# Decode block on one Trainium2 core: output in four transfers, GpSimd as closer, later load of x, spare matmuls

## Chip, cores, metric

One core of one Trainium2 chip runs the whole program. The metric is the device time in microseconds of one execution, as the median of several. The core's span in the profile is about 1.8 us shorter than the reported time. The update records of before show nearly every semaphore being written between 989.07 and 989.72 us, after the last instruction; that these writes make up the difference was not tested.

A transfer has three moments in what follows: its issue (an instruction on SyncE or ScalarE that starts it), its packets (moved by the 16 DMA engines), and its landing (the last update of the semaphore that tells the others that the data are there). In the profile lines PE is TensorE and PEld its weight loads, DVE is VectorE, ACT ScalarE, POOL GpSimd; SPq and ACTq are the issues of SyncE and ScalarE.

## The reference

One decode step of a transformer block with four sequences: attention over a cache of 4096 positions and 32 heads of 192, then a gated feed-forward layer.

```python
x = A_x                                              # [4, 1, 640]
h  = x + A_ref(layernorm(x), k_cache, v_cache, wq, wo)   # 32 heads, caches of 4 x 32 x 4096 x 192 bf16
h2 = h + B_ref(layernorm(h), w_gate, w_up, w_down)       # silu(x @ w_gate) * (x @ w_up) @ w_down
return h2                                            # [4, 1, 640] bf16
```

The two caches are 403 of the 424 MB that the kernel reads (4 x 32 x 4096 x 192 elements of two bytes, twice). The profile below shows that these loads set the time.

## The kernel before

The program is written as lists of operations for each engine with semaphore waits worked out from dependencies. Only its two ends matter here. At the start, x is loaded from ScalarE's queue while SyncE starts the first big load, wq:

```python
xd = dma("act", lambda e: e.dma_start(x16[:, :], x[:, 0, :].rearrange("b (n d) -> (b n) d", n=4)), S_x)
c1 = op("pool", ...)          # GpSimd: r32, then identF (c2), then masks
...                           # (cut) layer norm of x on VectorE, TensorE, ScalarE
wq_land = dma("sp", ... wqsb <- wq ..., S_wq)          # 7.9 MB, the first of the long stream on SyncE's queue
...                           # (cut) k and v of 32 units, then wo, w_gate, w_up, w_down, all on SyncE's queue
```

At the end come gate, up and down matmuls, each four column strips of 32 wide, then a cast out of PSUM and the output in two transfers of eight rows:

```python
for k, w in enumerate((wgsb, wusb)):
    for c in range(CD):                       # 5 column blocks; up arrives in two loads, 0-2 and 3-4
        for n in range(4):
            a = op("pe", ... PB[k][32*n:32*n+32, 0:FQ] += lnT[:, c, :].T @ w[:, c, n*FQ:(n+1)*FQ] ...)
    ...                                       # (cut) silu on ScalarE after gate
...                                           # (cut) product and transpose on VectorE -> guT
for c in range(CF):                           # 12 blocks; w_down arrives in three loads, 0-5, 6-9, 10-11
    for n in range(4):
        a = op("pe", ... psH[32*n:32*n+32, 0:DQ] += guT[:, c, :].T @ wdsb[:, c, n*DQ:(n+1)*DQ] ...)
a = op("dve", lambda e: e.tensor_copy(out=outsb[:, 0:DQ], in_=psH[:, 0:DQ]), [a])
fin = [dma(eng, lambda e, n=n: e.dma_start(
    out[:, 0, n * DQ:(n + 2) * DQ].rearrange("b (n d) -> n b d", n=2),
    outsb[32 * n:32 * n + 64:RB, 0:DQ]), S_out, [a]) for n, eng in ((0, "sp"), (2, "act"))]
with nc.Block(no_gpsimd_drain=True) as block:
    pr.emit(block, "act", fin[-1:])           # ScalarE waits for the output's semaphore, then all meet
```

The whole kernel may be printed here:

## Time and profile before

| | |
|---|---|
| time before, first three runs | 990.31 us median (990.21 to 990.85) |
| span of the profiled run | 988.36 us |
| HBM read | 424.29 MB |
| first data packet, last landing of w_down | 1.76 us, 985.01 us |

From the page of the kernel before: the DMA row (share of time in which the 16 DMA engines were busy, in tenths of 40 slices), and the DMA queue's totals.

```profile
DMA  9999999999999999999999999999999999999997
...
q1 hardware_dynamic: 10522, 424.29, 99.5%
...
HBM read 424.29 MB, written 0.01 MB: 429 GB/s over the span
```

The 16 engines are 90% busy or more in every slice but the last; the packets of queue q1 take 99.5% of their span. No compute engine is above 59% of the span. So a saving in the middle of the program should be worth little; the start of the stream and what follows its last byte are what can change the time.

The chain of waits of the kernel before, its last pieces in order (start us, duration us, what):

```profile
947.66 37.35 DMA wd_sb<-in_B_w_down_dram
985.01 0.04 issue
985.06 0.48 PE pb L573 x6
985.54 0.02 issue
985.57 0.33 DVE gu L576
```

The down weights land at 985.01, and only then can the last matmuls run. The chain as shown stops at the cast (L576), 2.5 us before the span's end. What comes after it are transfers, which the chain does not follow. They have to be read elsewhere: the issues from the timeline, here those of the kernel before (start, duration, engine, line),

```profile
985.92 0.68 SPq L577 DMA_DIRECT2D out_dram<-gu  x1
985.92 1.38 ACTq L577 DMA_DIRECT2D out_dram<-gu  x1
```

and packets and landings from the trace's records of DMA packets and of semaphore updates. That gives the tail of the kernel before, in three pieces that lead from the last landing of w_down to the end of the span:

| piece | us |
|---|---|
| last landing of w_down (985.01) to end of cast (985.89) | 0.88 |
| end of cast to last output landing (987.88) | 1.99 |
| last output landing to end of span (988.36) | 0.47 |

The middle piece is the longest, and its data are 5 KB. SyncE's first output packet moves 1.27 us after its issue began.

The stretches of the tail in the kernel before (stretch in us, its length, busy us and instructions of PE, PEld, DVE, ACT and POOL, then the granted TensorE clock, the DMA share and GB/s):

```profile
977.10:980.50 3.40, 1.33 (x16) 0.44 (x20) 0.00 (x0) 0.34 (x1) 0.00 (x0) 0.51 1.02 419
980.50:984.00 3.50, 1.64 (x32) 0.70 (x24) 1.41 (x2) 0.00 (x0) 0.00 (x0) 0.50 0.86 345
984.00:985.60 1.60, 1.18 (x24) 0.54 (x24) 0.03 (x1) 0.00 (x0) 0.00 (x0) 0.50 0.07 29
```

TensorE is busy less than half of each of the first two, and its clock is half (0.50) through the end. The clock records of this trace, which begin at 28.24 us, change only in steps of 3.413 us; these steps are called windows here. By the share of a window covered by matmul records, the 128 windows at full clock that were followed by full clock had 0.57 or more, and the 35 that were followed by half clock 0.54 or less. At half clock the 34 that were followed by full clock had 0.78 or more; the 84 others had 0.75 or less, but for one of 0.82.

### The profile page before, as it was taken

What the parts mean: (1) busy time and instruction counts of PE and PEld (TensorE: products, weight loads), DVE (VectorE), ACT (ScalarE), POOL (GpSimd) and SP (SyncE); (2) the same over time, 40 slices, a digit from 0 to 9 for tenths busy, and PEclk for the clock granted to TensorE, in tenths of its full rate; (3) what the DMA queues carried; (4) which work ended last, traced back from release to release, by engine and by line L of the source; (5) the groups of instructions that cost most, each with busy time, mean ns of one, the idle gap of its engine ahead of it and who ended that gap; (6) DMA issues with size and microseconds to landing.
All of it is one profiled execution on the core that took longest, in us unless ns stands there. A gap on an engine that the chain in (4) does not pass through costs nothing.

```text
span 988.4 us, 9462 instructions
## 1 busy us (share of the span) xinstructions
PE 581.5 (59%) x4409; PEld 128.6 (13%) x2941; DVE 552.6 (56%) x447; ACT 117.1 (12%) x376; POOL 3.6 (0%) x18
## 2 busy tenths in 40 slices
PE   1777555676555567545556654546765555675554
PEld 0001011111011111001111110111110111110023
DVE  1487545566655556655556665555666555566521
ACT  0311111100111110111111011111001111101120
POOL 1000000000000000000000000000000000000000
PEclk9788778887777888777788777778877778877776
DMA  9999999999999999999999999999999999999997
GB/s 403 426 440 424 438 436 428 436 430 436 436 428 438 430 434 436 428 438 432 432 436 428 438 432 432 436 428 438 432 432 436 428 438 434 430 436 428 440 429 327
DMA packets 10571, 424.39 MB, mean 429 GB/s; under 512 B 1220, under 2 KB 1220, under 8 KB 1732
## 3 DMA queue, kind: packets, MB, share of 16 engines
q1 hardware_dynamic: 10522, 424.29, 99.5%
q8 instruction: 5, 0.08, 0.0%
q10 hardware_dynamic: 42, 0.01, 0.0%
q14 instruction: 2, 0.02, 0.0%
HBM read 424.29 MB, written 0.01 MB: 429 GB/s over the span
## 4 chain that ended last, share of the span: by engine, by line
DMA 67%; PE 18%; DVE 12%; issue 1%; SPq 1%; DVEq 0%
DMA k<-in_A_k_cache_dram 64%; DVE prod L413 12%; PE pb L161 11%; PE pb L463 4%; DMA wd_sb<-in_B_w_down_dram 4%; PE pb L421 2%; SPq L366 0%; DVE sc L426 0%; PE pb L469 0%; DVEq L413 0%; SPq L392 0%; SPq L386 0%; PE pb L573 0%; PE pb L435 0%; SPq L331 0%
## 5 line engine op out<-in xcount | busy, mean ns | idle before, releaser
L413 DVE TENSOR_TENSOR prod<-k,qball 128x6144 f16<-128x6144 bf16 x128 | 426.4, 3352 | 220.1 <-DMA k<-in_A_k_cache_dram 220.1
L161 PE MATMUL pb<-prod,identH 128*128 128x512 f16 x1408 | 386.0, 431 | 0.0
L421 PE MATMUL pb<-prod,identH 128*128 128x512 f16 x128 | 57.9, 452 | 337.5 <-DVE prod L413 337.5
L426 DVE TENSOR_REDUCE sc<-pb 128x32 f32<-128x512 f32 x128 | 88.1, 688 | 108.7 <-PE pb L161 108.7
L478 ACT ACTIVATE otmp<-pb,minv 128x192 f32<-128x192 f32 x32 | 13.5, 421 | 649.1 <-PE pb L463 649.1
L421 PEld LDWEIGHTS pb<-prod,identH 128*128 128x128 f16 x128 | 13.2, 103 | 585.3 <-DVE prod L413 472.4
L463 PE MATMUL pb<-v,pbuf 128*8 128x384 bf16 x1984 | 86.0, 326 | 0.0
L454 ACT ACTIVATE pbuf<-sc,negM 32x128 bf16<-32x128 f32 x128 | 73.4, 574 | 4.9
L463 PEld LDWEIGHTS pb<-v,pbuf 128*8 128x8 bf16 x1984 | 45.4, 86 | 28.8
L482 DVE SCALAR_TENSOR_TENSOR orow<-pb,minv,otmp 128x192 f32<-128x192 f32 x32 | 13.4, 418 | 53.7 <-ACT otmp L478 53.7
L498 PEld LDWEIGHTS pb<-orow,here 128*128 128x128 f32 x256 | 33.5, 191 | 73.5 <-issue 71.1
L498 PE MATMUL pb<-orow,here 128*128 128x48 f32 x256 | 31.7, 267 | 1.1 <-DVE orow L482 1.1
L454 ACT ACTIVATION_READ_ACCUMULATOR pbuf<-sc,negM 32x1 f32 x128 | 31.8, 248 | 0.0
L448 ACT ACTIVATE negM<-pb 128x4 f32<-128x4 f32 x32 | 5.6, 174 | 160.2 <-PE pb L444 160.2
L469 PEld LDWEIGHTS pb<-lsb,headm 128*128 128x128 f32 x64 | 12.3, 194 | 74.8 <-issue 71.1
L444 PE MATMUL pb<-negMc,ones_row 1*128 1x4 f32 x64 | 12.2, 258 | 11.8 <-DVE negMc L439 11.8
L435 PE MATMUL pb<-identF,msb 128*1 128x128 f32 x64 | 12.1, 271 | 9.8 <-DVE msb L431 9.8
L439 DVE TENSOR_REDUCE negMc<-pb 1x4 f32<-1x128 f32 x32 | 8.9, 278 | 15.1 <-PE pb L435 15.1
L444 PEld LDWEIGHTS pb<-negMc,ones_row 1*128 1x128 f32 x64 | 9.4, 182 | 21.2 <-DVE negMc L439 21.2
L469 PE MATMUL pb<-lsb,headm 128*128 128x1 f32 x64 | 9.2, 213 | 2.7 <-ACT pbuf L454 2.7
L491 ACT ACTIVATE here<-place 128x131 f32 (+1 forms) x32 | 10.0, 312 | 0.9
L338 PE MATMUL pb<-wq_sb,lnT 128*32 128x384 bf16 x20 | 2.7, 520 | 12.1 <-DMA wq_sb<-in_A_wq_dram 12.1
(65 smaller groups left out, 91.1 us busy)
## 6 DMA issues: line engine op xcount, KB each, us to landing
k<-in_A_k_cache_dram SPq DMA_DIRECT2D x32, 6144.0 KB, 39.5
v<-in_A_v_cache_dram SPq DMA_DIRECT2D x31, 6144.0 KB, 25.5
wq_sb<-in_A_wq_dram SPq DMA_DIRECT2D x1, 7680.0 KB, 21.5
k<-in_A_v_cache_dram SPq DMA_DIRECT2D x1, 6144.0 KB, 39.8
wo_sb<-in_A_wo_dram SPq DMA_DIRECT2D x1, 5760.0 KB, 24.1
wo_sb<-in_A_wo_dram SPq DMA_DIRECT2D x1, 1920.0 KB, 26.1
wg_sb<-in_B_w_gate_dram SPq DMA_DIRECT2D x1, 1920.0 KB, 30.3
wu_sb<-in_B_w_up_dram SPq DMA_DIRECT2D x1, 1152.0 KB, 32.6
```

What stands on the lines that cost most here:

```text
L161: return e.add_instruction(mybir.InstMatmult(name=e.bass.get_next_instruction_name(), engine=mybir.EngineType.PE, start_tensor_calc=start, ...
L413: op("dve", lambda e: e.tensor_tensor(out=prod[BUF[k]][:, :, :], in0=kslot[u % 2][:, k * QT:(k + 1) * QT, :], in1=qball[:, bass.ds(u + pr. ...
L421: op("pe", lambda e, j=j: (e.matmul if j == 0 else partial(held_matmul, e))(psR[k][:, 0:QT * R], lhsT=identH[:, :], rhs=prod[BUF[k]][:, :, ...
L426: op("dve", lambda e: e.tensor_reduce(sc[u % 2][:, k * QT:(k + 1) * QT], psR[k][:, 0:QT * R].rearrange("q (t r) -> q t r", r=R), AX.X, ALU ...
L435: op("pe", lambda e: e.matmul(psS[0:1, XT], lhsT=msb[:, 0:1], rhs=identF[:, :], start=True, stop=True), [g("rmax", u), g("negM", u - 1), p ...
L444: op("pe", lambda e: e.matmul(psS[:, XB], lhsT=ones_row[0:1, :], rhs=negMc[0:1, :], start=True, stop=True), [g("hmax", u), g("negM", u - 1 ...
L454: op("act", lambda e, h=h, r=r: e.activation(out=pbuf[r, :, h], in_=sc[u % 2][r, :], func=ACTF.Exp, bias=negM[r, h:h + 1], scale=alpha, ac ...
L463: op("pe", lambda e, t=t, n=n: e.matmul(psO[32 * n:32 * n + 8, 0:2 * DH], lhsT=pbuf[:, t:t + 2, :].rearrange("q t m -> q (t m)"), rhs=vsrc ...
L469: op("pe", lambda e: e.matmul(psS[:, XL], lhsT=headm[:, :, :].rearrange("q r m -> q (r m)"), rhs=lsb[:, :], start=True, stop=True), [g("ex ...
L478: op("act", lambda e: e.activation(out=otmp[:, :], in_=psO[:, 0:DH], func=ACTF.Copy, scale=minv[:, 0:1]), [g("pv", u), g("minv", u), g("st ...
L482: op("dve", lambda e: e.scalar_tensor_tensor(out=orow[:, :], in0=psO[:, DH:2 * DH], scalar=minv[:, 1:2], in1=otmp[:, :], op0=ALU.mult, op1 ...
L498: op("pe", lambda e, i=i: e.matmul(psT[:, bass.ds(JW * at_unit(u)[0], JW)], lhsT=here[:, NI - 1 - i:NI - 1 - i + 128], rhs=orow[:, JW * i: ...
```

## The change

Four ideas. Smaller output transfers, so that each is done sooner, on two queues. GpSimd instead of ScalarE closes the program, since it collects the other engines at the end anyway (in the trace of before it takes over from ScalarE at 988.17 and lets the others go from 988.25). x waits until the identity matrix is built, which its first use needs too, and leaves the start of the stream to wq. Spare matmuls, whose results nobody reads, fill TensorE's waits so that its clock comes back to full before the last real ones.

```diff
-    xd = dma("act", ... x ..., S_x)
+    xd = dma("act", ... x ..., S_x, [lambda: c2])
...
+    def idle(n):
+        for _ in range(n):
+            op("pe", lambda e: e.matmul(PB[2][:, 0:256], lhsT=sel[:, 0, :], rhs=sel[:, 0:2, :].rearrange("q b m -> q (b m)"),
+                                        start=True, stop=True), [tk["rsum", NU - 1, NQ - 1]])
     for k, w in enumerate((wgsb, wusb)):
         for c in range(CD):
+            if c == 3 and k == 1:
+                idle(2)
...
+        idle(6 if k else 3)
...
     for c in range(CF):
+        if c == 6:
+            idle(3)
...
-    fin = [dma(eng, lambda e, n=n: e.dma_start(
-        out[:, 0, n * DQ:(n + 2) * DQ].rearrange("b (n d) -> n b d", n=2),
-        outsb[32 * n:32 * n + 64:RB, 0:DQ]), S_out, [a]) for n, eng in ((0, "sp"), (2, "act"))]
+    fin = [dma("sp" if n < 2 else "act", lambda e, n=n: e.dma_start(
+        out[:, 0, n * DQ:(n + 1) * DQ], outsb[32 * n:32 * n + 32:RB, 0:DQ]), S_out, [a]) for n in range(4)]
...
-        pr.emit(block, "act", fin[-1:])
+        pr.emit(block, "pool", fin[-1:])
```

More of the change, by code (lines that the diff above doesn't have):

```diff
@@ L270, in g @@
         return tk[key] if key[1] >= 0 else None
-    xd = dma("act", lambda e: e.dma_start(x16[:, :], x[:, 0, :].rearrange("b (n d) -> (b n) d", n=4)), S_x)
+    xd = dma("act", lambda e: e.dma_start(x16[:, :], x[:, 0, :].rearrange("b (n d) -> (b n) d", n=4)), S_x, [lambda: c2])
     c1 = op("pool", lambda e: e.memset(r32[:, :], 0.0))
```

## The prediction

> **What bounds the kernel.** The DMA stream. The page gives 424.39 MB at 429 GB/s; queue q1 is 99.5% of the 16 engines' span. In the packet records a 61,440-byte packet takes 2.267 us on every engine, 27.1 GB/s, so 424.39 MB need 978.8 us; the first packet starts at 1.76 us, the last w_down packet ends near 984.6, practically without idle. Compute counts only after the last landing. The chain of waits ends "DMA wd_sb"; the last w_down landing is 985.01. Then (timeline): eight down matmuls to 985.52, CAST to 985.90, output issues at 985.92 (SyncE 0.68 us, ScalarE 1.38 us), first output packets 987.19 (SyncE) and 987.46 (ScalarE), last landing 987.88, ScalarE's closing steps to 988.14, GpSimd's barrier, end at 988.4. The reported time is 1.8 us longer than the span. The change can touch only this 3.4 us tail and the start of the stream.
>
> **The steps.**
>
> 1. x after the identity. Its issue moves from 0.75 to about 3.1 us (identF ends 3.07). x lands at perhaps 9 to 10 us instead of 8.36; the layer norm takes 3.6 us and wq lands only at 22.3, so nothing waits. But the 16 engines start wq raggedly, from 1.76 to 3.21 us[...], and w_down's last chunk lands equally spread, 983.60 to 985.01[...].[...] Without x in between the last engine should start about 0.5 us sooner; I count -0.4 us on the critical path.
>
> 2. Spare matmuls (14 of 256 columns). The clock records change in steps of 3.413 us; the tail ran at half clock from 977.1. In this trace a window at full clock stayed there at 57% busy or more and fell at 54% or less; at half clock about 80% was needed to rise. The tail's windows had 34, 41, 46 and 35%. A spare costs about 0.21 us cold: three after gate bring 34% only to about 41%; the later ones may lift 46% over 80%. So full clock may return for the last down matmuls only, depending on the phase. Gain at most 0.2 us, on average 0.1. Risk: three cold spares (0.64 us) before column 6 start at 983.8 and delay its matmuls (984.28) by 0.1 to 0.2 us. Net -0.05.
>
> 3. Four output transfers. Four rows each instead of eight, but each queue issues twice, in series. ScalarE's 1.38 us look like waiting for SyncE's. A plain issue took 0.39 to 0.43 us elsewhere. If that holds here, the second pair starts 0.4 us later and the last landing slips: +0.15 us (range -0.3 to +0.8). The least certain term.
>
> 4. GpSimd closes. Saves ScalarE's branch, drain and hand-over (987.91 to 988.17): -0.15 us.
>
> Sum: -0.45 us, 989.8 us, range 988.9 to 990.6. Faster by over 2%: 0.5%; within 2%: 99%; slower: 0.5%.
>
> **What would show it.** Step 1: spread of first wq packets below 1.45 us, last w_down landing before 985.0. Step 2: clock after 975 us; time from last w_down landing to CAST, now 0.55 us. Step 3: CAST end to last output landing, now 1.98 us. Step 4: last landing to end of span, now 0.48 us.
>
> **What would make it wrong.** The ragged start may not come from x; an instruction fetch (16 KB packets[...]) may hit the latest engine; four issues may serialise at 0.7 us each and add a microsecond; the clock windows are phased differently in every run.

The four terms (-0.4, -0.05, +0.15, -0.15) sum to -0.45 us. The instruction fetch at 1.91 us in before took 1.28 us. The 0.21 us of a spare at half clock is an estimate by columns: in the trace of before the eleven matmuls of 512 columns from 695.30 us on, at half clock, start 0.427 us apart, so 256 columns take about 0.21.

## The result, and the profile after

The changed kernel takes 991.54 us (median of 6 runs, 991.27 to 991.82); before, 990.44 us (6 runs, 990.21 to 990.85). It is 1.1 us slower, outside the predicted 988.9 to 990.6. The ratio is 1.001 (95% interval 0.9998 to 1.0023). The interval is wide beside what is at stake, but the two sets of six runs don't overlap, and the trace shows where the microsecond is.

The DMA queue's line of the page after, the end of its chain, and the output issues:

```profile
q1 hardware_dynamic: 10528, 424.29, 99.4%
```

```profile
948.15 37.21 DMA wd_sb<-in_B_w_down_dram
985.37 0.04 issue
985.41 0.35 PE pb L583 x8
985.76 0.02 issue
985.78 0.32 DVE gu L586
```

```profile
986.13 1.39 SPq L587 DMA_DIRECT2D out_dram<-gu  x2
986.14 1.90 ACTq L587 DMA_DIRECT2D out_dram<-gu  x2
```

The stream is as full as before. The last matmuls take 0.35 us instead of 0.48. The two queues now spend 1.39 and 1.90 us on issuing. Each queue's two issues, by the view of the output tensor (count, then shortest, median and longest ns, first and last start):

```profile
L587 SPq DMA_DIRECT2D out_dram<-gu x2: 593/672/750, 986.1 to 986.9; - x2
L587 ACTq DMA_DIRECT2D out_dram<-gu x2: 596/935/1274, 986.1 to 987.4; - x2
```

The stretches after, with the same lengths of about one clock window:

```profile
977.70:981.10 3.40, 2.01 (x22) 0.56 (x22) 0.00 (x0) 0.02 (x1) 0.00 (x0) 0.50 1.02 414
981.10:984.50 3.40, 3.17 (x40) 1.69 (x33) 1.41 (x2) 0.00 (x0) 0.00 (x0) 0.50 0.71 286
984.50:985.80 1.30, 1.04 (x27) 0.38 (x24) 0.02 (x1) 0.00 (x0) 0.00 (x0) 0.99 0.02 8
```

The spares fill the second stretch to 3.17 of 3.40 us, and the clock is full (0.99) for the last matmuls.

In the pieces of the tail:

| piece | before | after | difference |
|---|---|---|---|
| start of span to last landing of w_down | 985.01 | 985.37 | +0.35 |
| to end of cast | 0.88 | 0.74 | -0.14 |
| to last output landing | 1.99 | 3.00 | +1.01 |
| to end of span | 0.47 | 0.37 | -0.10 |
| span | 988.36 | 989.48 | +1.12 |

(Differences from three decimals.) The output is 1.0 us of the 1.1. Its records say how. The four issues begin at 986.13 (SyncE), 986.14 (ScalarE), 986.93 (SyncE) and 987.45 (ScalarE); their first packets start at 987.48, 987.57, 988.16 and 988.69; the last landing is 989.10. Each takes 1.23 to 1.44 us from the begin of its issue to its first packet, and the packets themselves less than 0.1 us. The second issue on each queue began only when the first had ended (0.05 and 0.03 us after it), so it comes 0.80 us later on SyncE and 1.31 us later on ScalarE, and pays its 1.24 us of latency from there.

Theory A is thus: what counts is when the last issue begins. Rivals: (B) the shape, four rows a transfer (with four closing packets of 4 bytes each, where a transfer of eight rows had two), is slow in itself; (C) the loss is the later w_down, brought by the move of x; and, for the 0.35 us, chance.

### The profile page after: what moved, and what is told of

The parts are those of the page before. It is cut to its first block, busy times and chain, and to the rows that moved or that the text cites. A ratio compares the mean times of both kernels' runs of the same rounds, so it can differ in the third digit from the quotient of the medians. Undisturbed runs are those within 1.5% of the kernel's fastest.

```text
span 989.5 us, 9491 instructions
## 1 busy us (share of the span) xinstructions
PE 582.1 (59%) x4422; PEld 129.7 (13%) x2955; DVE 552.5 (56%) x447; ACT 117.0 (12%) x376; POOL 3.6 (0%) x18
## 4 chain that ended last, share of the span: by engine, by line
DMA 67%; PE 18%; DVE 12%; issue 1%; SPq 1%; DVEq 0%
DMA k<-in_A_k_cache_dram 64%; DVE prod L413 12%; PE pb L161 11%; PE pb L463 4%; DMA wd_sb<-in_B_w_down_dram 4%; PE pb L421 2%; SPq L366 0%; DVE sc L426 0%; PE pb L469 0%; DVEq L413 0%; SPq L392 0%; SPq L386 0%; PE pb L435 0%; SPq L331 0%; PE pb L583 0%
```

## The experiments

Each job's kernels ran on the same chip in turn with runs of the kernel before. The pieces of the tail of every profiled run come first, in us; the experiments follow.

| run | last landing of w_down | to end of cast | to last output landing | to end | median, and that of before |
|---|---|---|---|---|---|
| a_four_out | 985.33 | 0.88 | 2.99 | 0.47 | 991.72, 990.55 |
| a_x_late | 985.14 | 0.88 | 2.00 | 0.47 | 990.36, 990.55 |
| a_spares | 985.07 | 0.74 | 2.00 | 0.47 | 990.22, 990.55 |
| a_pool_close | 985.00 | 0.88 | 2.00 | 0.37 | 990.55, 990.55 |
| b_half_out | 985.51 | 0.88 | 1.98 | 0.47 | 990.36, 990.48 |
| b_eight_out | 986.57 | 0.88 | 4.67 | 0.47 | 993.94, 990.48 |
| b_one_out_pool_spares | 985.38 | 0.74 | 1.80 | 0.37 | 990.09, 990.48 |
| b_wq_wait | 986.63 | 0.88 | 2.00 | 0.47 | 992.06, 990.48 |
| c_after_two_out | 985.06 | 0.88 | 2.01 | 0.37 | 990.43, 990.52 |
| c_four_sp | 984.96 | 0.88 | 3.71 | 0.46 | 992.04, 990.52 |
| c_one_act | 985.02 | 0.88 | 1.80 | 0.47 | 990.59, 990.52 |
| d_one_out_pool_dense | 985.11 | 0.74 | 1.80 | 0.37 | 989.91, 990.67 |

The three pieces after the landing repeat to about 0.02 us wherever the same part is present. The first column does not: leaving out b_wq_wait it goes from 984.96 to 986.57, though up to there the kernels issue the same loads in the same order (only x's moment differs).

### a_four_out: the four output transfers alone

```diff
-    fin = [dma(eng, ... 8 rows ...) for n, eng in ((0, "sp"), (2, "act"))]
+    fin = [dma("sp" if n < 2 else "act", ... 4 rows ...) for n in range(4)]
```

> Only the four output transfers, added to the kernel before. Theory A (issues of output transfers are served one after another, so two more of them push the last landing back): end of the CAST to last output landing goes from 1.99 us to 2.9-3.1 us as in the changed kernel, time +0.9 to +1.1 us over before. Theory B (the loss came from the later last landing of w_down, that is from moving x or from chance): 2.0-2.2 us there, time within 0.3 us of before.

Measured: 2.99 us, and the median 1.17 us over before (991.46 to 991.74 against 990.15 to 990.92). Theory A's number. The issues repeat those of the profile after:

```profile
L577 SPq DMA_DIRECT2D out_dram<-gu x2: 592/670/749, 986.2 to 987.0; - x2
L577 ACTq DMA_DIRECT2D out_dram<-gu x2: 595/934/1274, 986.2 to 987.5; - x2
```

This part alone gives the whole loss.

### a_x_late: x after the identity, alone

```diff
-    ... S_x)
+    ... S_x, [lambda: c2])
```

> Only x loaded after the identity. The prediction's step 1 says -0.4 us and a first-packet spread of wq under 1.45 us. Theory after the result: the spread comes from a 16 KB instruction fetch that sits in front of wq's packet on one DMA engine, x has no part in it: spread stays 1.4-1.5 us, time within 0.2 us of before. Rival: moving x makes the last engine later (the changed kernel's last w_down landing was 0.35 us later): time +0.3 to +0.4 us, and spread of the last w_down landings over 2 us.

Measured: the first wq packets start over 1.28 us (1.78 to 3.06), against 1.45 in before; the last landing of w_down is 985.14; the median is 0.19 us under before, with overlapping ranges. There is no loss, so rival C falls; and no gain of the predicted 0.4 us is to be seen. The spread is a little under the prediction's 1.45 and under my 1.4 to 1.5, but other kernels that load x early spread by the same 1.29 us (a_spares, a_pool_close), so x is not what makes it.

### a_spares: the spare matmuls alone

```diff
+    def idle(n): ...                    # 3 after gate, 2 inside up, 6 after up, 3 inside down
```

> Only the spare matmuls. If full clock comes back before the last down matmuls as in the changed kernel: last w_down landing to end of CAST 0.72-0.76 us instead of 0.88, time -0.1 to -0.2 us. If the phase of the 3.4 us windows decides and this run missed it: 0.88 us, and time 0 to +0.1 us.

Measured: 0.74 us, as expected where full clock comes back in time. In this run it came back at 985.05, just before the last matmuls. The median is 0.33 us lower, of which the trace shows 0.14.

### a_pool_close: GpSimd as closing engine alone

```diff
-        pr.emit(block, "act", fin[-1:])
+        pr.emit(block, "pool", fin[-1:])
```

> Only GpSimd as the closing engine. Last output landing to end of span 0.37-0.39 us as in the changed kernel, against 0.48; time -0.1 us. If the gain in the changed kernel came with the other output order instead, no change (0.48).

Measured: 0.37 us against 0.47. The median is equal to that of before: 0.10 us is not to be seen in medians here.

### b_half_out: two transfers of four rows (wrong)

```diff
-    fin = [dma(eng, ... 8 rows ...) for n, eng in ((0, "sp"), (2, "act"))]
+    fin = [dma(eng, ... 4 rows ...) for n, eng in ((0, "sp"), (2, "act"))]
```

> Kernel before with only two of the four output transfers of four rows, one from SyncE and one from ScalarE (half of the output is left unwritten: wrong on purpose). If the cost is the number of issues per queue: end of CAST to last output landing 1.9-2.1 us, as with two transfers of eight rows. If the shape of four rows[...] is what costs: 2.4 us or more.

Measured: 1.98 us. Half of the output is missing. The shape costs nothing that shows, so rival B falls, and the number of issues is left.

### b_eight_out: eight transfers of two rows

```diff
+    fin = [dma("sp" if n < 2 else "act", ... 2 rows ...) for n in range(4) for h in range(2)]
```

> Kernel before with eight transfers of two rows, four from each queue. If each further issue on a queue costs its 0.6-0.8 us in series: ScalarE's fourth issue starts about 2.5-2.7 us after its first, CAST end to last landing 4.0-4.6 us, time +2.0 to +2.6 us over before. If both queues have to take turns for the whole of every issue: 5 us or more. If the cost comes once with a second issue and not with every one: 3.0 us.

Measured: 4.67 us, a little over the expected 4.0 to 4.6. The issues of the eight (shortest, median and longest ns, first and last start):

```profile
L577 SPq DMA_DIRECT2D out_dram<-gu x4: 563/571/737, 987.5 to 989.5; - x4
L577 ACTq DMA_DIRECT2D out_dram<-gu x4: 581/704/1439, 987.5 to 990.3; - x4
```

Every further issue costs its 0.56 to 0.71 us on its queue. ScalarE's fourth begins 2.82 us after its first; its first packet follows at 991.65 and the last landing at 992.12. The two queues overlap: SyncE's four issues took 2.57 us in all and ScalarE's 3.52, both from 987.48, where turns for the whole of every issue would have taken the sum, 6.1. The median rose by 3.5 us, more than the 2.7 us of the tail piece and than expected; in the profiled run the last landing of w_down was late as well (986.57), for which no run gives a reason. There even the mean of its sixteen landings was 0.4 us later than in the other kernels without the wait (984.49 against 984.04 to 984.16), so this is more than the scatter described below.

### b_one_out_pool_spares: one transfer, with the two parts that gain

```diff
+    fin = [dma("sp", lambda e: e.dma_start(
+        out[:, 0, :].rearrange("b (n d) -> n b d", n=4), outsb[0:128:RB, 0:DQ]), S_out, [a])]
```

> The other direction: one transfer of all 16 rows from SyncE, GpSimd closes, spare matmuls kept, x as in before. If the number of issues decides: first packet about 1.3 us after the issue, CAST end to last landing 1.65-1.75 us (before 1.99); with 0.74 us from last w_down landing to CAST end and 0.37 us at the end, the sum after the last w_down landing is 2.80 us against 3.34 in before: time -0.4 to -0.6 us, the fastest of all. If ScalarE's share of the work matters (both queues help each other), the landing comes at 2.0 us or later and the gain is only 0.2 us.

Measured: 1.80 us, and 2.92 us in all after the last landing of w_down, against 3.34 in before: 0.43 us less, and a median 0.39 us less (990.09 against 990.48; its runs 989.87 to 990.28). Its one issue:

```profile
L587 SPq DMA_DIRECT2D out_dram<-gu x1: 703/703/703, 986.2 to 986.2; - x1
```

Going to fewer transfers gains, as going to more loses. The output's piece is 0.19 us shorter and not 0.24 to 0.34 as expected: the first packet came 1.31 us after the issue, as expected, but 16 rows on one queue need 0.13 us of packets and the landing 0.34 more.

### b_wq_wait: the stream starts after the instruction fetch

```diff
-    wq_land = dma("sp", ..., S_wq)
+    wq_land = dma("sp", ..., S_wq, [c1])
```

> Kernel before with the first big load (wq) held back until GpSimd's fifth operation (about 2.4 us), so that the 16 KB instruction fetch at 1.9 us and x go through idle DMA engines. If the late engine at the start is the one with the fetch: the first wq packets then spread by 1.0 us or less instead of 1.3-1.45. And if the stream is never idle, the 1.7 us of later start appear nearly whole at the end: time +1.2 to +1.8 us over before. If some slack in the stream absorbs it: within 0.4 us.

This one is about the failed step 1. The packet records of before show a packet of 16,384 bytes of the kind "instruction" at 1.91 us for 1.28 us, and the last of the sixteen first wq packets starts at 3.21, 0.02 us after it ended. In 11 of the 13 profiled runs without this wait (before and after among them) the last start lies within 0.03 us of the end of such a fetch, whether that is at 2.93 or at 4.27 us; in a_x_late and c_after_two_out it lies 0.16 and 0.37 us behind it. Measured with the wait: first wq packets from 3.41 to 4.37, a spread of 0.96 us as expected, though x still loads early; and the landings of wq spread by 1.36 us, where those of the three other kernels of the same job spread by 2.42 to 2.50. Their fetches were long (1.72 to 2.15 us). In before, from another job, the landings of wq spread by 1.35 too, so the start and not this figure is the evidence: without its last engine, before starts over 1.00 us, as this run does. So the late engine at the start is very probably the one with the fetch; the kept records do not name a packet's engine, and the times alone say so. The median rises by 1.58 us. The first of the sixteen starts 1.65 us later, their mean 1.50 us later and the last 1.17 us later; the landings of w_down come 1.44 us later in the mean and 1.62 us at the last. So little in the stream absorbs a later start. The run explains the spread and is no gain.

### c_after_two_out: the change without its four transfers

```diff
-    fin = [dma("sp" if n < 2 else "act", ... 4 rows ...) for n in range(4)]
+    fin = [dma(eng, ... 8 rows ...) for n, eng in ((0, "sp"), (2, "act"))]
```

> The changed kernel with its four output transfers taken back to the two of before. If the four transfers are the whole loss and the other parts give 0.14 (spares) and 0.10 us (GpSimd closes): CAST end to last landing 2.00 us, last w_down landing to CAST end 0.74 us, last landing to end 0.37 us, time -0.1 to -0.4 us against before. If moving x costs something: 0 or a loss.

Measured: 2.01 us, as before, and the loss is gone (990.43 against 990.52). But the spares missed: 0.88 us. Three stretches of this run:

```profile
976.00:979.40 3.40, 3.07 (x35) 1.16 (x31) 0.00 (x0) 0.49 (x1) 0.00 (x0) 0.51 0.99 409
979.40:982.80 3.40, 1.88 (x24) 0.74 (x16) 1.40 (x2) 0.00 (x0) 0.00 (x0) 0.99 1.00 405
982.80:986.20 3.40, 2.67 (x51) 1.52 (x51) 0.32 (x1) 0.00 (x0) 0.00 (x0) 0.52 0.25 101
```

Here the window boundaries lay 1.6 us earlier than in the profile after. The clock rose at 979.5, the same matmuls then took less time and filled only 1.88 us of the next window, and the clock fell again at 982.9, before the last matmuls. So the spares' gain depends on the phase of the windows.

### c_four_sp: all four from SyncE

```diff
+    fin = [dma("sp", ... 4 rows ...) for n in range(4)]
```

> Kernel before with the four transfers all from SyncE. If a queue serves its own issues in series and the two queues help each other: SyncE's fourth issue begins 1.9-2.1 us after the first, CAST end to last landing 3.5-3.8 us (2.99 with two queues), time +1.5 to +1.8 us over before.[...]

Measured: 3.71 us, and 1.52 us over before in the median. The issues:

```profile
L577 SPq DMA_DIRECT2D out_dram<-gu x4: 577/585/750, 985.9 to 987.9; - x4
```

The fourth begins 2.05 us after the first. Two queues do help (2.99 against 3.71, so the second queue was worth 0.72 us). The other branch, the same 2.9 to 3.1 us whatever the queue, falls. But one queue with four issues is far worse than one with one (1.80).

### c_one_act: one transfer from ScalarE

```diff
+    fin = [dma("act", ... 16 rows ...)]
```

> Kernel before with one transfer of 16 rows from ScalarE alone. If the 1.27-1.39 us of ScalarE's first issue are a wait for SyncE's issue of the same moment: it takes 0.7 us now, first packet 1.3 us after its start, CAST end to last landing 1.80 us as from SyncE alone. If ScalarE is simply slower at issuing: 1.2 us or more, landing at 1.9-2.1 us.

Measured: neither branch. The issue:

```profile
L577 ACTq DMA_DIRECT2D out_dram<-gu x1: 1134/1134/1134, 985.9 to 985.9; - x1
```

It takes 1.13 us with no other issue about, where SyncE's takes 0.70; so most of ScalarE's 1.38 us in before was not a wait for SyncE. Nor is ScalarE simply slow: where it issues several, only the first is long (1.27 us, then 0.60 us in the changed kernel; 1.44, then 0.58 to 0.71 us in b_eight_out), and its second in the changed kernel took as long as SyncE's (0.59). What makes its first one long was not tested. Yet its first packet comes 1.30 us after the begin and the last landing at 1.80 us, exactly as from SyncE. The longer issue is no loss for that transfer, only for the next one on the queue. The median does not show the 0.19 us (990.59 against 990.52).

### d_one_out_pool_dense: one transfer, denser spares

```diff
-        idle(6 if k else 3)             # and idle(2) inside up
+        idle(8)                         # and idle(3) inside up
```

> The best combination so far (one transfer of 16 rows from SyncE, GpSimd closes, x as before) with denser spare matmuls: eight after the gate matmuls, three inside up, eight after up, three inside down. If the spares' gain depends on the phase of the 3.4 us clock windows because the row of matmuls was too thin, a denser row gives full clock at the end in more of the runs: last w_down landing to CAST end 0.74 us, CAST end to last landing 1.80 us, end 0.37 us, time -0.4 to -0.5 us against before. If the denser spares get in the way of the real matmuls, or full clock comes too early and falls again: 0.88 us or more, and time -0.3 us or worse.

Measured: 0.74, 1.80 and 0.37 us, 989.91 us in the median against 990.67 (989.74 to 990.32 against 990.20 to 991.06); ratio 0.9993, interval 0.9979 to 1.0006. The three stretches, to be compared with those of c_after_two_out, whose windows had nearly the same phase:

```profile
976.00:979.40 3.40, 3.40 (x28) 1.52 (x27) 0.00 (x0) 0.49 (x1) 0.00 (x0) 0.51 1.01 420
979.40:982.80 3.40, 2.57 (x32) 1.26 (x31) 1.40 (x2) 0.00 (x0) 0.00 (x0) 1.00 0.98 398
982.80:986.20 3.40, 1.82 (x51) 1.02 (x51) 0.32 (x1) 0.00 (x0) 0.00 (x0) 0.99 0.23 91
```

With 2.57 us of work in the second stretch the clock stayed full to the end, in the phase in which the thinner row lost it. One profile shows that; how often it holds was not measured. Of the 0.76 us of the medians the tail explains 0.42 (2.92 against 3.34); the rest is in the scatter described next.

## Why the prediction was wrong

The direction and the size failed in one term, and a second term had a wrong cause.

**Step 3, four output transfers: predicted +0.15 us, measured +1.00.** The step as put was: a plain issue took 0.39 to 0.43 us elsewhere (many took 0.33), "If that holds here, the second pair starts 0.4 us later". It does not hold. The second issue began 0.80 us after the first on SyncE and 1.31 us on ScalarE, since the first ones took 0.75 and 1.27 us. The last issue sets the last landing: begin plus 1.24 us to the first packet plus 0.41 to the last landing. (From the begin of the issue to the first packet it was 1.02 us for wq and 1.23 to 1.54 us for the outputs of before and after.) The borrowed durations were of transfers on all 128 partitions, or of the 16 rows of x; the better models were in the same trace, 0.68 and 1.38 us for the very outputs that were to be split, and they were there in the prediction as observed numbers. ScalarE's 1.38 us were argued away as "waiting for SyncE's"; c_one_act shows 1.13 us without SyncE. Taken at their face the two durations would have given a second issue about 1.4 us later on ScalarE, and a loss of about 1 us. The prediction named that ("four issues may serialise at 0.7 us each and add a microsecond") but only as a risk.

Why the short issues take 0.33 to 0.44 us and these 0.56 to 0.75 us on SyncE was not settled. The traces show one difference: the two output transfers of before have four closing packets and six semaphore updates, the four of the changed kernel sixteen and twenty, so one update more than packets for each transfer; x has sixteen of both, and its issue took 0.41 us. No run changed only that.

**Step 1, x later: predicted -0.4 us, measured none.** Half of the observation was right: sixteen engines start raggedly (1.76 to 3.21 us in before), and much of the lateness stays (in b_half_out and b_one_out_pool_spares the sixteen landings of a load spread by 2.4 to 2.6 us all the way from wq at 22 us to the last k at 924). But it does not stay as it is: in before the last load of w_down spread by 1.65 us, from 983.36 and not from 983.60 as the prediction read, so it was not "equally spread". The cause named, x in between, was wrong. The first wq packets were as ragged without it (1.76 to 3.21 us in the changed kernel, to the hundredth that of before), and by its timing the late engine is the one that serves a 16 KB instruction fetch (in before it ended at 3.19 us, and the last first packet of wq came at 3.21), which took 0.95 to 2.15 us at the start of these runs. The prediction named such fetches, and that x might not be the cause, only under what would make it wrong.

**Step 2, spares: predicted -0.05, measured -0.14 us where they work.** The forecast held in its outline, with the windows' phase as said: of five profiles with spares, four had full clock at the end and one of the thinner rows did not. The bounds of 57, 54 and 80% are those of the trace of before. Other traces do not keep them: at full clock a window of 0.57 fell in the changed kernel and one of 0.67 in b_eight_out, and one of 0.43 stayed in d_one_out_pool_dense; at half clock one of 0.90 in a_spares did not rise. So either the share is not the whole rule, or records of matmuls are missing there. The delay of column 6's matmuls happened (they began 0.14 us after their data at 984.61 in the changed kernel) but cost nothing, since the last data came later still.

**Step 4, GpSimd closes: predicted -0.15, measured -0.10 us.** Right in the path, a little too large in size.

**The rest.** The terms sum to +0.77 us in the tail (1.01 - 0.14 - 0.10). The measured difference of the medians is 1.10, and that of the two profiles 1.12, of which 0.35 is the later last landing of w_down. It is a matter of the latest engine alone: the mean of the sixteen landings of w_down is 984.16 in before and 984.08 in the changed kernel, so the stream as a whole was not slower. What makes the latest one differ was not shown. The times say only that the spread between engines jumps about where small instruction fetches lie. Between the loads of k that landed at 50 and at about 515 us, the distance from the first to the last engine grew from 1.47 to 2.27 us in the changed kernel, and from 1.34 to 1.56 in before; fetches of 16 and 8 KB lie at 62, about 101 and about 109 us in both. In the changed kernel and in a_four_out, which loads x early, the jump comes between the landings at 95 and 110 us (1.66 to 2.19, 1.55 to 2.04), long before any output, so this jump is neither x's doing nor a delay by the output transfers. It does not go with the number of output transfers: the last landing was 985.33 with four transfers on two queues, 984.96 with four on one, 985.51 with two halves, 985.38 with one. But a_four_out and the profile after are both on the late side, and whether that is chance stays open (the added instructions could also shift the fetches; no run tests it).

## What to carry to other kernels

At the end of this program nothing hid an issue: the latency counted from the last one (in the changed kernel 1.24 us to its first packet and 0.41 more to the last landing; an issue took 0.59 to 0.75 us on SyncE, a transfer's packets less than 0.1), so send a small result in one transfer (here 1.80 us against 1.99 with two and 2.99 with four). Splitting it may pay where the pieces are ready at different times; that was not tried. Cost a new instruction by the nearest twin in the trace (same queue, same direction, same shape), not by the cheapest of its kind, and don't explain a long twin away without a test. Where a stream of DMA has no idle, look at the latest of the engines and not at their mean, and read small effects from the pieces of the trace that repeat, not from medians that scatter more than the effect.
